# Attention, experts and a Strassen network on one core: conversions one operation at a time, four of them in the network, x split in halves

## The chip, the cores and the metric

The kernel runs on one core of a Trainium2 chip. The metric is the device time of one execution in microseconds (us). Five engines work side by side, each through its own instructions in the order in which they are recorded: TensorE (PE; its weight loads are PEld), VectorE (DVE), ScalarE (ACT), GpSimd (POOL) and SyncE (SP, which issues most DMAs). An instruction starts when its engine has finished the one before and when what it waits for is there.

## The reference, cut to what matters

```python
x = attention(q, k, v, tau)                 # 4 batches, 8 heads, 576 positions, width 64
x = x.reshape(2304, 512)
e = argmax(xn @ en.T / tau)                 # one of 8 experts for each token, gate g
y = relu(x @ w1[e]) @ w2[e]                 # w1: 512 x 1024, w2: 1024 x 512 for each expert
h = (g * y) @ w_in                          # 512 x 2048
out = (max(h, 0) + alpha * min(h, 0)) @ w_out   # 2048 x 512
```

The inputs are float64 in memory; w_in and w_out come to the core as pairs of 32-bit words, and have to be turned into a high and a low part.

## The kernel before, in words

The program has three stretches. **Attention** takes the first 345 us; the change does not touch it. **Experts** (function `experts`, to about 609 us) goes through 64 steps g, eight for each expert. In a step PE makes twelve products of the first layer (`l1`, L1225) and twelve of the second (`l2`, L1256 to L1258) for the step before. Each product is made of three matmuls (high by high, high by low, low by high), so every operand is split: ACT copies the high part, DVE or POOL subtracts the low one (`wsplit`, L1123/L1124 and L1137/L1138; `relu`, L1208 and L1209; `xprep`, L1175/L1176). `l2` waits for L1209, the low part of h.

Between them the same engines prepare the network. `conv` (L1620) turns a 128 x 512 block of w_in or w_out into 32-bit numbers: one ACT operation (L1605), five on DVE (L1606, L1607, L1609, L1613, L1614), and for w_in one POOL addition (L1646), for w_out an ACT copy (L1612) and two POOL operations (L1617, L1618). `CVG` lists the steps g at which one starts; it is a generator, and the loop decides how much of it is recorded at a time. There are 16 blocks of w_in and four of w_out. `early` is a list of due steps: sums and splits of w_in's blocks (`sums`, `factor`), the loads of x (`fetch`), its differences and splits (`diff`, `split`), on tiles of 128 x 768.

**The network** (function `near_network`, 609 to 1010 us) multiplies x by w_in in Strassen's way, with seven products (`PROD`) in place of eight. It makes six visits (`VISITS`): a visit takes one third q of the tokens and one half h of the 16 blocks f of the hidden width, in four pairs i. In a pair PE makes seven products of six matmuls (`prod`, L1869) into the banks ha and hb, and four groups of nine matmuls of the second layer (`f2mm`, L1985 to L1987). ACT copies ha away (`held`, L1878), DVE adds (L1891), `act` applies the leaky relu (ACT L1895/L1896 and DVE L1897, or in visits 3 to 5 DVE alone, L1900/L1902), ACT makes the high part gh (L1913) and POOL the low part gl (L1918). PE can go on with ha only when ACT has copied it.

Beside this stand chains of small steps: `tick` records after each PE group the next steps of each chain, as far as a budget for each engine allows (`room`); a step "N" does nothing and costs a place, and a change of engine within a chain costs one too. `finish` records what is left of a chain at once, where its result is needed. Chains are `wout` (a block of w_out, due in a certain pair), `factors` (the products' weights of one pair of w_in, with stores to DRAM, L2041, L2045, L2047), and at the end of visits 0, 1, 3 and 4, when x moves to another third, the differences and splits of the next x (`after`, `xsplit`). At the very end three blocks of the second layer's rows are stored by indirect DMAs that POOL issues (`put`, L1950).

Of the kernel before, what the change touches and what calls it, by code (L numbers as in the profile page):

```python
# [44 lines left out]
CVG = {False: [21 * i // 8 for i in range(KF2 + 4)], True: [4 * i for i in range(15)] + [59, 61]}  # L45
# [7 lines left out]
NV = 4  # L53
# [159 lines left out]
def attn_moe_ffn(ctx: ExitStack, tc, q, k, v, tau, emb, mtau, w1, w2, w_in, w_out, alpha, out):  # L213
# [843 lines left out]
    def experts(CAPS, general, y2):  # L1057
# [466 lines left out]
        for g in range(NE * KF + 1):  # L1524
# [3 lines left out]
            wsplit(1, g + LA1)  # L1528
            for x in todo:
                for _ in x:  # L1530
                    pass
            todo = []
# [25 lines left out]
    def shared(st, general):  # L1558
# [61 lines left out]
        def conv():  # L1620
# [12 lines left out]
            for group in ((0,), (1, 2, 3), (4,) if hl is not None else ()):  # L1633
                for x in group:
                    steps[x]()
                if group:
                    yield
            for x in steps[5 if hl is not None else 4:]:
# [83 lines left out]
        def diff(p, eng):  # L1722

            b11, b21, b12, b22 = raws()
            if p < 3:
                RAW["t", p] = t = cv_p.tile([128, KD // 2 * HB], F32, tag=f"t{p}", name=f"t{p}", bufs=1)
            if p == 1:
                eng.tensor_tensor(t, b12, b11, op=ALU.subtract)
            elif p == 2:
                eng.tensor_tensor(t, b22, RAW["t", 1], op=ALU.subtract)  # L1730
            elif p == 3:
                eng.tensor_tensor(b12, b22, b12, op=ALU.subtract)
            else:
                eng.tensor_tensor(RAW["t", 2], b21, RAW["t", 2], op=ALU.subtract)

        def split(p, eng):
            b11, b21, b12, b22 = raws()
            src = {1: b11, 2: b21, 6: RAW.get(("t", 2)), 7: b12, 5: RAW.get(("t", 1)), 3: b22, 4: RAW.get(("t", 2))}[p]
# [3 lines left out]
            yield  # L1742
            eng.tensor_tensor(t[:, 1], src, t[:, 0].bitcast(F32), op=ALU.subtract)
# [18 lines left out]
        for i in range(NQH):  # L1762
            g0 = 10.5 * i + 4.0
# [12 lines left out]
        for x, (kind, p, e) in enumerate((("s", 1, V), ("d", 1, G), ("s", 2, G), ("d", 3, V), ("d", 2, G), ("s", 7, V),  # L1776
                                          ("s", 6, V), ("s", 5, G), ("d", 4, G))):
            if kind == "d":
                at(g0 + 0.75 * x, lambda p=p, e=e: diff(p, e))
            else:  # L1780
                f = run(lambda p=p, e=e: split(p, e))
                at(g0 + 0.75 * x, f)
                at(g0 + 0.75 * x + 0.8, f)
# [534 lines left out]
```

## Time and profile before

| what | value |
| --- | --- |
| three timed runs | 1019.30, 1016.85 and 1019.21 us, median 1019.21 us |
| the profiled execution's own time | 1021.06 us |
| its span (first to last instruction) | 1019.2 us |
| mean granted TensorE clock | 0.981 |
| busy: PE, PEld, DVE, ACT, POOL | 961.3, 887.6, 797.7, 618.6, 684.9 us |

A row of the timeline reads: start and duration in us, engine, line, operation, what it writes and reads, how many; in brackets the engine's idle time before it and what ended that. A row of the waits reads: the waiting instruction, who it waited for, us in total, how many times, the longest. The rows that matter stand in the section below.

### The profile page before, as it was taken

How to read it: one execution, taken by the hardware profiler on the slowest of the kernel's cores; microseconds unless marked ns; L12 is line 12 of the kernel's file. 1: busy time of each engine (PE TensorE's matmuls, PEld its weight loads, DVE VectorE, ACT ScalarE, POOL GpSimd, SP SyncE). 2: the span in 40 equal slices, each digit the busy share in tenths (PEclk: the TensorE clock that was granted, in tenths of full speed). 3: DMA queues.
4: the chain of work that ended last, by engine and by line, in shares of the span. 5: the costliest groups of instructions: out<-in, count | busy, mean ns of one | idle time of the engine just before them, and what ended most of it. 6: DMA issues, size and time to landing. Idle time of an engine off the chain costs nothing. (4 is left out here: it accounts for less than half of the span.)

```text
span 1019.2 us, 18395 instructions
## 1 busy us (share of the span) xinstructions
PE 961.3 (94%) x6099; PEld 887.6 (87%) x6099; DVE 797.7 (78%) x1431; ACT 618.6 (61%) x1419; POOL 684.9 (67%) x654
## 2 busy tenths in 40 slices
PE   7999999899999599998998999999899999999995
PEld 6899999899999499998997998989788888798884
DVE  7999999999999688988999777874963567738633
ACT  6989999799998345655556456665565523324120
POOL 6988899899998433655889465747764647636523
PEclk7999999999999799999999999999999999999998
DMA  2333555534451477988989766557476655464641
GB/s 74 104 95 82 140 153 180 162 105 134 123 156 65 167 272 246 319 272 265 280 271 262 244 170 194 191 193 266 157 270 215 233 164 167 156 216 146 195 135 66
DMA packets 119160, 186.06 MB, mean 183 GB/s; under 512 B 24024, under 2 KB 50936, under 8 KB 119056
## 3 DMA queue, kind: packets, MB, share of 16 engines
q1 hardware_dynamic: 115184, 174.48, 55.1%
q0 software_dynamic: 3456, 9.59, 2.5%
q8 instruction: 51, 0.84, 0.3%
q10 hardware_dynamic: 416, 0.72, 0.2%
q14 instruction: 53, 0.43, 0.1%
HBM read 127.48 MB, written 48.41 MB: 173 GB/s over the span
## 5 line engine op out<-in xcount | busy, mean ns | idle before, releaser
L1918 POOL TENSOR_TENSOR gl<-c,gh 128x384 fp32r<-128x384 f32 x96 | 109.1, 1140 | 139.9 <-ACT gh L1913 122.1
L446 POOL TENSOR_TENSOR ptl<-x,pth 128x512 fp32r<-128x512 f32 x97 | 124.8, 1288 | 6.8
L1869 PE MATMUL ha<-x,wr 128*128 128x384 f32 x576 | 119.1, 342 | 5.9 <-ACT d L1878 3.9
L650 DVE SCALAR_TENSOR_TENSOR p<-s,mx,e 128x576 f32<-128x576 f32 x144 | 116.6, 812 | 7.2 <-ACT mx L638 3.2
L1987 PE MATMUL o<-wo,gl 128*128 128x512 f32 x288 | 115.2, 400 | 4.0 <-POOL gl L1918 4.0
L1869 PEld LDWEIGHTS ha<-x,wr 128*128 128x128 f32 x576 | 104.3, 190 | 16.6 <-ACT d L1878 5.5
L1225 PE MATMUL l<-x,w 128*128 128x256 f32 (+6 forms) x744 | 118.7, 308 | 0.0
L1986 PE MATMUL o<-wo,gh 128*128 128x512 f32 x288 | 114.7, 398 | 2.2 <-POOL wo L1618 2.2
L634 DVE TENSOR_REDUCE mx<-s 128x1 f32<-128x576 f32 x144 | 108.5, 754 | 8.3 <-PE s L627 5.2
L663 PE MATMUL t<-ident,p 128*128 128x128 f32 (+1 forms) x720 | 112.3, 277 | 2.2 <-ACT x L689 0.9
L1985 PE MATMUL o<-wo,gh 128*128 128x512 f32 x288 | 113.6, 394 | 0.0
L1225 PEld LDWEIGHTS l<-x,w 128*128 128x128 f32 x744 | 110.7, 188 | 0.6
L643 ACT ACTIVATE e<-s,mx 128x576 f32<-128x576 f32 x144 | 106.3, 739 | 7.1 <-DVE mx L634 6.0
L1869 PE MATMUL hb<-x,wr 128*128 128x384 f32 x432 | 87.8, 338 | 2.4 <-DVE c L1891 2.3
L1913 ACT CAST gh<-c 128x384 fp32r<-128x384 f32 x96 | 48.9, 514 | 66.5 <-DVE c L1902 47.0
L663 PEld LDWEIGHTS t<-ident,p 128*128 128x128 f32 (+1 forms) x720 | 81.1, 138 | 8.5 <-DVE p L650 2.4
L1257 PE MATMUL y<-h,w 128*128 128x256 f32 (+6 forms) x256 | 80.4, 314 | 6.9 <-DVE h L1209 6.7
L627 PE MATMUL s<-ks,qs 128*128 128x288 f32 x256 | 82.7, 338 | 2.4 <-ACT qs L534 1.4
L1208 ACT ACTIVATE h<-l 128x256 fp32r<-128x256 f32 (+6 forms) x64 | 28.3, 442 | 92.3 <-PE l L1225 90.7
L1256 PE MATMUL y<-h,w 128*128 128x256 f32 (+6 forms) x256 | 82.3, 321 | 2.0 <-ACT yT L1268 1.6
L1869 PEld LDWEIGHTS hb<-x,wr 128*128 128x128 f32 x432 | 76.9, 190 | 3.8 <-DVE c L1891 3.7
L1258 PE MATMUL y<-h,w 128*128 128x256 f32 (+6 forms) x256 | 79.1, 309 | 0.0
(274 smaller groups left out, 2649.1 us busy)
## 6 DMA issues: line engine op xcount, KB each, us to landing
wr<-ws SPq DMA_DIRECT2D x168, 256.0 KB
stg<-in_moe_w_dram SPq DMA_DIRECT2D x34, 512.0 KB
stg<-in_moe_w_dram SPq DMA_DIRECT2D x15, 1024.0 KB
kx<-ks SPq DMA_DIRECT2D x60, 144.0 KB
xd<-zt SPq DMA_DIRECT2D x33, 256.0 KB
raw<-yt_d SPq DMA_DIRECT2D x10, 768.0 KB
ws<-wr SPq DMA_DIRECT2D x28, 256.0 KB
ws<-wf SPq DMA_DIRECT2D x28, 256.0 KB
```

Source lines behind the costliest of these rows:

```text
L446: lambda: nc.gpsimd.tensor_tensor(lo, raw, hi.bitcast(F32), op=ALU.subtract))
L627: nc.tensor.matmul(s[:, hf, 0:288], lt, st[nm, a][:, hf * 288:(hf + 1) * 288], start=(j == 0 and x == 0), stop=(j == n - 1 and x == 1))
L634: nc.vector.tensor_reduce(out=mx[:, 0:1], in_=st["s", t][:, :, 0:288], op=ALU.min, axis=AX.XY)
L643: nc.scalar.activation(e, st["s", t][:, :, 0:288], AF.Exp, bias=st["mx", t][:, 0:1], scale=-1.0)
L650: nc.vector.scalar_tensor_tensor(out=p.rearrange("q (a b) -> q a b", a=2), in0=st["s", t][:, :, 0:288], scalar=st["mx", t][:, 2:3], in1=st ...
L663: nc.tensor.transpose(m[0:w, j * n + i * 128:j * n + (i + 1) * 128], st["p", t][:, c * 128:c * 128 + w], ident)
L1225: nc.tensor.matmul(m[:, 0:n], w[:, a, c], st["x"][:, b, c, 0:n], start=(i == 0), stop=(i + 1 == len(terms)))
L1869: nc.tensor.matmul(m, w[:, a, k], x[:, b, k], start=start and n == 0, stop=n + 1 == len(terms), skip_group_check=not start)
L1918: P.tensor_tensor(gl, c, gh.bitcast(F32), op=ALU.subtract)
L1985: nc.tensor.matmul(m, gh[:, ts], WO[f][:, 0, :], start=first and x == 0, stop=False)
L1986: nc.tensor.matmul(m, gh[:, ts], WO[f][:, 1, :], start=False, stop=False)
L1987: nc.tensor.matmul(m, gl[:, ts], WO[f][:, 0, :], start=False, stop=n[0] == full and x + 1 == len(gs))
```

## The change

In the experts a conversion is recorded one operation at a time, two places in a step g, instead of in runs of three and two or more; 16 start there instead of 20, every 3.33 steps instead of every 2.63. Four blocks of w_in (c = 12 to 15) are converted in the network instead, by a new chain `win` in visits 1 and 2. The sums and splits of w_in's blocks come at other steps. In the network, differences and splits of x are made in halves; differences 1 to 3 for the next x move to DVE and start a pair earlier, and difference 4 goes into another tile. The chain behind `act` gets one more empty step before the high part. In the last two pairs of visits 3 and 4 `act` uses the form with two ACT operations. Blocks of w_out start at other pairs. At the end the last three high and low parts are recorded before the groups that lead to the stores.

```diff
-CVG = {False: [21 * i // 8 for i in range(KF2 + 4)], True: ...}
+CVG = {False: [10 * i // 3 for i in range(16)], True: ...}
...
             for x in todo:
-                for _ in x:
-                    pass
-            todo = []
+                next(x, None)
...
             if g in CVG[general]:
                 todo.append(conv())
-                next(todo[-1])
-                next(todo[-1])
...
+            if not general:
+                for x in todo:
+                    next(x, None)
...
-            cvq = [(1, 2 * i + x) for h in range(NQH) for i in (h, NQH + h) for x in range(2)] + [(2, c) for c in range(NV)]
+            cvq = [(1, 2 * i + x) for i in (0, NQH, 1, NQH + 1, 2, 3) for x in range(2)] + [(2, c) for c in range(NV)]
...
+            for n, x in enumerate(steps):
                 x()
-            cvload()
+                if n == (5 if hl is None else 6):
+                    cvload()
+                yield
...
-        def diff(p, eng):
+        def diff(p, eng, half):
...
+            o, x, y = {1: (t1, b12, b11), 2: (t2, b22, t1), 3: (b12, b22, b12), 4: (b11, b21, t2)}[p]
+            n = slice(half * HB, (half + 1) * HB)
+            eng.tensor_tensor(o[:, n], x[:, n], y[:, n], op=ALU.subtract)
...
             nc.scalar.copy(t[:, 0], src)
-            yield
-            eng.tensor_tensor(t[:, 1], src, t[:, 0].bitcast(F32), op=ALU.subtract)
+            for half in range(2):
+                yield
+                n = slice(half * HB // 2, (half + 1) * HB // 2)
+                eng.tensor_tensor(t[:, 1, :, n], src[:, :, n], t[:, 0, :, n].bitcast(F32), op=ALU.subtract)
...
-            g0 = 10.5 * i + 4.0
+            g0 = (8.0, 21.0, 34.5, 45.0)[i]
...
-            if v < 3:
+            if v < 3 or busy:
...
-            chain(0, first + join + [("A", 0.52, halves), ("P", 1.12, low)], ("g", v, f, hf), 1)
+            chain(0, first + join + [("N", 0, nothing), ("A", 0.52, halves), ("P", 1.12, low)], ("g", v, f, hf), 1)
...
+        def win(c):
...
+            chain(3, [("W", 0, lambda: len(open_) < 2), ("S", 0, load)] + [("N", 0, nothing)] * 3 + [("A", 0.67, begin)]
+                  + [("V", t, lambda k=k: x["steps"][k + 1]()) for k, t in enumerate((0.75, 0.75, 1.2, 0.5, 0.75))]
+                  + [("P", 1.4, add), ("N", 0, nothing), ("S", 0, store)], ("c", c))
...
-                if i == NQH - 2 and p == 1:
+                if i == 1 and p == 1:
...
-                          + [("N", 0, nothing)] * 5 + [("P", 2.15, lambda: diff(1, P)), ("V", 1.0, lambda: diff(3, V)),
-                                                       ("P", 2.15, lambda: diff(2, P))], "fetch")
+                          + [("N", 0, nothing)] * 5 + [x for d in (1, 3, 2) for half in range(2) for x in (
+                              ("V", 0.6, lambda d=d, half=half: diff(d, V, half)), ("N", 0, nothing))], "fetch")
...
-        work = {0: [("o", NV + x, 0) for x in range(NQH)], 1: [("f", NQH, 0), ("f", NQH + 1, 2)] + [("o", 8 + x, x) for x in range(3)],
-                2: [("f", NQH + 2, 0), ("f", NQH + 3, 2), ("o", 11, 0), ("o", 12, 3)], 3: [("o", 13, 0), ("o", 14, 1), ("o", 15, 2)]}
+        work = {0: [("o", NV, 0), ("o", NV + 1, 0), ("o", NV + 2, 1), ("o", NV + 3, 2)],
+                1: [("f", NQH, 0), ("c", 2 * NQH + 4, 0), ("f", NQH + 1, 1), ("c", 2 * NQH + 5, 1), ("o", 8, 2)],
+                2: [("f", NQH + 2, 0), ("c", 2 * NQH + 6, 0), ("c", 2 * NQH + 7, 0), ("o", 9, 1), ("o", 10, 1), ("f", NQH + 3, 2),
+                    ("o", 11, 2), ("o", 12, 3)],
+                3: [("o", 13, 0), ("o", 14, 1), ("o", 15, 2)]}
...
+                busy = moving(v) and i >= 2
...
+        for f, hf in ((f1, 1), (f0, 1), (f1, 0)):
+            finish(("g", v, f, hf))
         f2mm(v, (f1,), 1)
         f2mm(v, (f0,), 1)
```

The first place is DVE in the experts, expert 5 (272 tokens), around one conversion of w_out; x7s is the conversion's tile, h the low part that PE waits for. Before:

```order
L1138 TENSOR_TENSOR w2_8273<-stg2_8111,w2_8273 128x512
L1606 TENSOR_SCALAR x7s_8294<-x7s_8294 128x512
L1607 TENSOR_SCALAR x7s_8294<-x7s_8294 128x512
L1609 SCALAR_TENSOR_TENSOR x7s_8294<-x2s_8058,x7s_8294 128x512
L1209 SCALAR_TENSOR_TENSOR h_8312<-l1_8299,h_8312 128x272
L1124 TENSOR_TENSOR w1_8315<-stg1_8054,w1_8315 128x512
L1613 TENSOR_SCALAR x7s_8294<-x7s_8294 128x512
L1614 SCALAR_TENSOR_TENSOR x7s_8294<-x2s_8058,x7s_8294 128x512
L1176 TENSOR_TENSOR x0_8216<-x_8325,x0_8216 128x320
L1209 SCALAR_TENSOR_TENSOR h_8368<-l1_8355,h_8368 128x272
```

And now:

```order
L1616 TENSOR_SCALAR x7s_8170<-x7s_8170 128x512
L1176 TENSOR_TENSOR x0_8137<-x_8195,x0_8137 128x320
L1138 TENSOR_TENSOR w2_8201<-stg2_8041,w2_8201 128x512
L1617 TENSOR_SCALAR x7s_8170<-x7s_8170 128x512
L1209 SCALAR_TENSOR_TENSOR h_8238<-l1_8225,h_8238 128x272
L1124 TENSOR_TENSOR w1_8241<-stg1_7987,w1_8241 128x512
L1619 SCALAR_TENSOR_TENSOR x7s_8170<-x2s_7941,x7s_8170 128x512
L1176 TENSOR_TENSOR x0_8137<-x_8245,x0_8137 128x320
L1209 SCALAR_TENSOR_TENSOR h_8289<-l1_8276,h_8289 128x272
L1124 TENSOR_TENSOR w1_8292<-stg1_7987,w1_8292 128x512
L1623 TENSOR_SCALAR x7s_8170<-x7s_8170 128x512
```

Three operations of the conversion stood together ahead of one h; now one or two stand between one h and the next.

The second place is POOL in the last pair of visit 0. wo7 is the block of w_out that PE needs first in the next visit, x2 and x5 are splits, t2 and raw the targets of difference 4. Before:

```order
L1743 TENSOR_TENSOR x2_9690<-raw_9495,x2_9690 128x768
L1918 TENSOR_TENSOR gl_9714<-c_9670,gh_9713 128x384
L1617 TENSOR_TENSOR f_9540<-f_9540,wo7_9542 128x512
L1734 TENSOR_TENSOR t2_9642<-raw_9495,t2_9642 128x768
L1743 TENSOR_TENSOR x5_9746<-t1_9596,x5_9746 128x768
L1918 TENSOR_TENSOR gl_9788<-c_9742,gh_9787 128x384
L1918 TENSOR_TENSOR gl_9802<-c_9768,gh_9801 128x384
L1618 TENSOR_TENSOR wo7_9542<-f_9540,r_9541 128x512
L1918 TENSOR_TENSOR gl_9839<-c_9784,gh_9838 128x384
```

And now:

```order
L1627 TENSOR_TENSOR f_9523<-f_9523,wo7_9525 128x512
L1932 TENSOR_TENSOR gl_9641<-c_9579,gh_9640 128x384
L1745 TENSOR_TENSOR raw_9291<-raw_9291,t2_9520 128x384
L1932 TENSOR_TENSOR gl_9655<-c_9593,gh_9654 128x384
L1756 TENSOR_TENSOR x2_9674<-raw_9291,x2_9674 128x2x192 x2
L1932 TENSOR_TENSOR gl_9697<-c_9637,gh_9696 128x384
L1745 TENSOR_TENSOR raw_9291<-raw_9291,t2_9520 128x384
L1756 TENSOR_TENSOR x5_9720<-t1_9386,x5_9720 128x2x192 x2
L1628 TENSOR_TENSOR wo7_9525<-f_9523,r_9524 128x512
L1932 TENSOR_TENSOR gl_9776<-c_9715,gh_9775 128x384
L1932 TENSOR_TENSOR gl_9796<-c_9743,gh_9795 128x384
```

The last operation on wo7 (L1618, now L1628) stands ahead of the two gl that it stood behind. Differences 1 and 2, which POOL made shortly before (L1728, L1730), are gone from its order.

The third place is ACT at the start of visit 0, from the copy of ha that follows the fifth product. Before:

```order
L1878 COPY d_9248<-ha_9185 128x384
L1913 CAST gh_9253<-c_9211 128x384
L1605 ACTIVATE f_9256<-cr_9198 128x512
L1895 ACTIVATE u_9269<-ha_9185 128x384
L1896 ACTIVATE c_9268<-ha_9185 128x384
L1895 ACTIVATE u_9251<-c_9250 128x384
```

And now:

```order
L1892 COPY d_9215<-ha_9150 128x384
L1615 ACTIVATE f_9220<-cr_9163 128x512
L1615 ACTIVATE f_9224<-cr_9165 128x512
L1909 ACTIVATE u_9237<-ha_9150 128x384
L1910 ACTIVATE c_9236<-ha_9150 128x384
L1927 CAST gh_9250<-c_9176 128x384
```

The first gh stood directly behind the copy; now four operations come first, two of which wait for PE's sixth product.

## Rows read from the trace of the kernel before

**Rows 1.** The page, busy time of PE: us, share of the span, instructions.
```profile
PE 961.3 (94%) x6099; PEld 887.6 (87%) x6099; DVE 797.7 (78%) x1431; ACT 618.6 (61%) x1419; POOL 684.9 (67%) x654
```
**Rows 2.** Waits of PE in the network, 600 us to the end.
```profile
PE o L1987 <- POOL gl L1918: 4.0, 3, 3.1
PE ha L1869 <- ACT d L1878: 3.9, 3, 1.8
PE hb L1869 <- DVE c L1891: 2.3, 3, 1.1
PE o L1986 <- POOL wo L1618: 2.2, 1, 2.2
PE ha L1869 <- DVE c L1902: 2.0, 2, 1.3
```
**Rows 3.** Waits of PE in the experts, 400 to 600 us.
```profile
PE y L1257 <- DVE h L1209: 6.5, 7, 1.5
PE y L1256 <- ACT yT L1268: 1.6, 1, 1.6
PE y L1256 <- ACT w L1137: 0.4, 1, 0.4
```
**Rows 4.** Windows: stretch, length, busy PE, PEld, DVE, ACT, POOL, clock, DMA, GB/s.
```profile
470.00:490.00 20.00, 16.39 (x125) 15.60 (x124) 19.66 (x35) 10.11 (x23) 10.71 (x10) 1.00 0.80 252
...
670.00:680.00 10.00, 7.78 (x31) 6.53 (x30) 5.69 (x7) 5.05 (x10) 5.54 (x4) 0.83 0.36 138
...
750.00:760.00 10.00, 8.23 (x35) 7.39 (x34) 5.75 (x9) 8.25 (x18) 4.55 (x5) 0.83 0.85 293
...
750.00:800.00 50.00, 48.23 (x233) 43.12 (x232) 22.11 (x36) 28.91 (x65) 23.93 (x26) 0.97 0.72 239
```
**Rows 5.** Timeline of the experts, around two of PE's waits for h.
```profile
474.73 1.20 DVE L1295 TENSOR_TENSOR be<-be,sm 128x64 f32<-128x64 f32 x1
...
476.57 0.38 PE L1257 MATMUL y<-h,w 128*128 128x256 f32 x1 [1.51 <-DVE h L1209]
...
542.90 1.70 DVE L1609 SCALAR_TENSOR_TENSOR x7s<-x2s,x7s 128x512 uint32<-128x512 uint32 x1
...
545.00 0.39 PE L1257 MATMUL y<-h,w 128*128 128x272 f32 x1 [1.51 <-DVE h L1209]
```
**Rows 6.** Timeline of visits 0 to 2, the steps that hold PE up.
```profile
646.14 2.29 POOL L1728 TENSOR_TENSOR t<-raw 128x768 f32<-128x768 f32 x1
...
671.25 1.58 POOL L1618 TENSOR_TENSOR wo<-f,r 128x512 fp32r<-128x512 f32 x1
...
716.90 2.60 DVE L1732 TENSOR_TENSOR raw<-raw 128x768 f32<-128x768 f32 x1
...
750.21 0.40 ACT L2041 CAST wf<-sum 128x256 fp32r<-128x256 f32 x1 [2.23 <-DMA ws<-wf]
```
**Rows 7.** Timeline of the end.
```profile
999.53 0.51 ACT L1913 CAST gh<-c 128x384 fp32r<-128x384 f32 x1 [1.75 <-DVE c L1902]
...
1002.12 0.98 POOL L1950 DMA_INDIRECT out_dram<-os,gs  x1 [0.30 <-DVE os L1931]
...
1004.38 1.02 POOL L1918 TENSOR_TENSOR gl<-c,gh 128x384 fp32r<-128x384 f32 x1
1005.46 0.79 PE L1987 MATMUL o<-wo,gl 128*128 128x512 f32 x1 [3.14 <-POOL gl L1918]
...
1011.12 0.97 POOL L1950 DMA_INDIRECT out_dram<-os,gs  x1 [0.41 <-POOLq L2281]
```
**Rows 8.** Groups of equal instructions in the network: us busy, mean ns of one.
```profile
L1918 POOL TENSOR_TENSOR gl<-c,gh 128x384 fp32r<-128x384 f32 x96 | 109.1, 1140 | 139.9 <-ACT gh L1913 122.1 <-PE hb L1869 14.0 <-PE ha L1869 2.0
```
**Rows 9.** Timeline of visit 0's start.
```profile
612.25 0.56 DVE L1891 TENSOR_TENSOR c<-hb,v 128x384 f32<-128x384 f32 x1 [1.71 <-PE hb L1869]
...
612.75 0.96 DVE L1743 TENSOR_TENSOR x<-raw,x 128x768 fp32r<-128x768 f32 x1
...
617.33 0.49 ACT L1895 ACTIVATE u<-ha 128x384 f32<-128x384 f32 x1 [0.42 <-PE ha L1869]
```
**Rows 10.** Timeline of the end, POOL's low part and PE's use of it.
```profile
995.74 1.01 POOL L1918 TENSOR_TENSOR gl<-c,gh 128x384 fp32r<-128x384 f32 x1 [5.06 <-ACT gh L1913]
...
997.26 0.39 PE L1987 MATMUL o<-wo,gl 128*128 128x512 f32 x1
```

More of the change, by code (lines that the diff above doesn't have):

```diff
@@ L43 @@
 WARM2 = 18
-CVG = {False: [21 * i // 8 for i in range(KF2 + 4)], True: [4 * i for i in range(15)] + [59, 61]}
+CVG = {False: [10 * i // 3 for i in range(16)], True: [4 * i for i in range(15)] + [59, 61]}
 CV2 = (8, 14, 20)
@@ L1551, in experts @@
                 todo.append(conv())
-                next(todo[-1])
-                next(todo[-1])
+                if general:
+                    next(todo[-1])
+                    next(todo[-1])
+            if not general:
+                for x in todo:
+                    next(x, None)
+        for x in todo:
+            for _ in x:
+                pass
         for i in range(len(ntile(NE - 1))):
@@ L1882, in near_network, with act @@
         acts = []
-        def act(v, f, hf, m, w=None):
+        def act(v, f, hf, m, w=None, busy=False):
             if len(acts) > 2:
@@ L2021, in wout, with load, begin, add @@
                   + [(e, t, lambda k=k: nth(k + 1)) for k, (e, t) in enumerate(kinds)], ("wo", c))
+        def win(c):
+            x = {}
+            def load():
+                open_.append(("c", c))
+                x["raw"] = raw = cw_p.tile([128, 1024], U32, tag="cr", name="cr", bufs=2)
+                nc.sync.dma_start(raw.rearrange("p (k f) -> p k f", k=2), y2["cvsource"](1, c))
+            def begin():
+                f, r = x["fr"] = [cw_p.tile([128, 512], U32, tag=nm, name=nm, bufs=2) for nm in ("f", "r")]
+                x["steps"] = [y[2] for y in y2["cvsteps"](x["raw"], f, r, None)]
+                x["steps"][0]()
+            def add():
+                f, r = (t.bitcast(F32) for t in x["fr"])
+                P.tensor_tensor(f, f, r, op=ALU.add)
+            def store():
+                i, half = divmod(c, 2)
+                nc.sync.dma_start(wa_d[i - NQH][:, half * DM:(half + 1) * DM], x["fr"][0].bitcast(F32))
+                open_.remove(("c", c))
+            chain(3, [("W", 0, lambda: len(open_) < 2), ("S", 0, load)] + [("N", 0, nothing)] * 3 + [("A", 0.67, begin)]
+                  + [("V", t, lambda k=k: x["steps"][k + 1]()) for k, t in enumerate((0.75, 0.75, 1.2, 0.5, 0.75))]
+                  + [("P", 1.4, add), ("N", 0, nothing), ("S", 0, store)], ("c", c))
         def factors(i):
@@ L2049, in next_ @@
                     made.remove(i)
-            steps = [("W", 0, lambda: not made), ("S", 0, load)] + [("N", 0, nothing)] * 3
+            steps = [("W", 0, lambda: not made and not any(x["name"] in (("c", 2 * i), ("c", 2 * i + 1)) for x in chains)),
+                     ("S", 0, load)] + [("N", 0, nothing)] * 3
             steps += [("V", 0.8, lambda k=k: nth(k)) for k in range(4)] + [("N", 0, nothing)]
@@ L2062, in hi @@
                 next(x["g"])
-            chain(2, [("A", 0.85, hi), (e, 1.05 if e == "V" else 2.15, lambda: next(x["g"], None))], ("x", p))
+            chain(2, [("A", 0.85, hi)] + [(e, 0.6 if e == "V" else 1.1, lambda: next(x["g"], None))] * 2, ("x", p))
         def moving(v):
@@ L2112, in near_network @@
                     if when == i:
-                        (wout if kind == "o" else factors)(x)
+                        {"o": wout, "f": factors, "c": win}[kind](x)
                 if h and q != VISITS[2][0] and i == NQH - 2:
@@ L2128, in near_network @@
                 prod(v, i, 2, b, True)
-                act(v, f0, 0, b, d1)
+                act(v, f0, 0, b, d1, busy)
                 step(2)
@@ L2140, in near_network @@
                 d3 = held("d", a)
-                act(v, f1, 1, b, d3)
+                act(v, f1, 1, b, d3, busy)
                 step(5)
```

55 lines of the change are left out of this document (29 added, 26 removed).

## The prediction

> **What bounds the kernel now.** I read the page's busy times first: PE is busy for 961.3 of 1019.2 us [rows 1]. No engine can shorten that work here, since the change removes no matmul; what can go is time in which PE waits, and time in which its clock is down. So I read next who ends PE's waits. In the network they sum to 4.0 + 3.9 + 2.3 + 2.2 + 2.0 = 14.4 us, in five groups of two or three waits each [rows 2]: a low part gl from POOL, a copy of ha from ACT, an addition on DVE, a block of w_out from POOL, and DVE's half of the activation. In the experts they are 8.5 us, 6.5 of them in seven waits for DVE's low part of h [rows 3]. Third, the windows: between 470 and 490 us DVE is busy 19.66 of 20 us, so there it is itself the bound; and two stretches of 10 us in the network have a granted clock of 0.83 [rows 4]. Those two hold the waits of 2.2 for w_out and of 1.8 for ACT's copy, and PE ran at the lower of its two levels for a while after each. A loss of 17% of 10 us is 1.7 us each, so 3.4 us more hang on these two waits. Together 14.4 + 8.5 + 3.4 = 26.3 us could go at most from these places, all but the stores behind PE's last work, which I take apart. Then I read single steps, to see what stands in front of each wait.
>
> **Experts.** Two waits of 1.51 us are the longest [rows 5]. At 545.00 the cause is a conversion's operation of 1.70 us right before the low part of h; it was one of three recorded together. The change leaves one or two between one h and the next, so this kind goes. At 476.57 it is `be`, a step of the mixing weights of 1.20 us, and its neighbours; these don't move, and while DVE is at 19.66 of 20 us a shorter run only hands the lateness on. I take the seven waits for h and the one for yT (ACT, whose w_out copy stood between DVE's operations), 8.1 us, and let 4.7 go: somewhat over half. The ends: nothing gained, if DVE is full throughout, and 7 us, if all but the wait on `be` (and the small one for w) goes. Four conversions fewer take work off DVE there; that is worth nothing by itself where PE isn't waiting, and its help is in the 4.7. **Gain 4.7 (0 to 7).**
>
> **The block of w_out (wo7).** PE waited 2.2 us for L1618 of 1.58 us at 671.25 [rows 6], with 1.7 us of clock behind it. In the new order this operation stands ahead of two gl that it stood behind, and differences 1 and 2, of which the row at 646.14 shows one with 2.29 us on POOL, are gone from that queue. The differences alone are up to 4.6 us, the wait was 2.2, so it goes whole. What is late next: the two gl behind it; PE has other groups to do before it needs them. **Gain 3.9 (0 to 3.9).**
>
> **ACT's copies of ha.** Three waits, 3.9 us, and 1.7 of clock behind the longest. That one comes from the factors: a copy into wf waited 2.23 us for a transfer, the store of the previous wf, and the copy of ha stood behind it on ACT [rows 6]. The change does not take the store away. It moves the chain's place, and adds traffic to visits 1 and 2: four loads of raw words and four stores, where the DMA engines already show 0.72 over 750 to 800 and 0.85 between 750 and 760 [rows 4]. Of 5.6 us I let 3.0 stand, half of the two shorter waits (2.1) and 2.0 of the longest with its clock: **gain 2.6 (-1.5 to 5)**, the lower end being one more such wait on a store with nothing else saved.
>
> **DVE's additions and activations at the ends of moving visits.** Five waits, 4.3 us. The row at 716.90 shows why: a difference of 128 x 768 took 2.60 us on DVE, and what PE needed stood behind it [rows 6]. Halves put at most half of this ahead of it, and in the last two pairs of visits 3 and 4 ACT takes two operations of the activation over from DVE. Against it stands that differences 1 and 2 now are DVE's. They start a pair earlier, where DVE has room (22.11 busy of 50 us between 750 and 800, a stretch without a moving x [rows 4]). **Gain 3.2 (0 to 4.3)**; the loss is a rival below.
>
> **The end.** Six stores are issued by POOL, and they set the last instruction: the first at 1002.12 took 0.98, the last begins at 1011.12. Between them POOL makes the gl for which PE waited 3.14 us, at 1004.38, 1.02 long, though its gh had begun at 999.53 and taken 0.51 [rows 7]. POOL's order put stores ahead of gl. The change records gl first: then it ends near 1001.1, and six stores follow, at steps of about 1.3 (0.98 and what lies between: an estimate, from 0.98 plus the 0.30 and 0.41 of idle time that these rows show). The last begins at 1001.1 + 5 x 1.3 = 1007.6 in place of 1011.12. PE's last groups would begin some 4 us earlier, so they don't take its place as the bound. **Gain 3.5 (2.5 to 4.7)**, the upper end if the stores are no longer held by anything but their issue.
>
> **What it costs.** First, the empty step behind `act` delays each of the 96 groups of gh and gl by a place. POOL's gl lasts 1.14 us on average and its queue mostly waits for gh (139.9 us of idle time) [rows 8], so POOL is not late by itself; the delay falls on the margin between gl and its use. At the start of visit 0 this margin is smallest: gh used to stand right behind a copy, and now four ACT operations come first, two of them, the casts of conversions, beside u and c, which wait for PE's next product (617.33 shows such a wait, 0.42 [rows 9]). I take 2.2 us there (0 to 4, the top being two waits of about 2: four operations of the 0.49 of that row). Second, elsewhere: at the end a gl was finished at 995.74 + 1.01 = 996.75 and used at 997.26, a margin of 0.5, with no first product between [rows 10]; in the steady pairs two products stand between, so most stay hidden. There I count with the four conversions that now lie in visits 1 and 2 (DVE five operations each, ACT and POOL one each, hidden in a DVE that is busy 44% of the time there) and with blocks of w_out that start later. I take 2.0 us for all of it (0 to 6; the top is one wait of 0.5 in each of about 12 pairs). Third, the halves: on DVE, 128 x 384 took 0.56 us and 128 x 768 took 0.96 [rows 9], so two halves cost 0.16 more; a visit's end has eight halved operations on DVE, and four ends make 32 x 0.16 = 5.1 us. I count it at nothing, hidden beside PE. If the cover is gone, it is paid. **Cost 4.2 (0 to 10).**
>
> The Trainium skill speaks against the halves: its page "Perfetto Trace Analysis", section "Optimizing Scalar/DVE Operations", says that grouping into larger operations improves throughput if the engine is saturated, and only where it is not, but causes bubbles elsewhere, does breaking instructions up help. The rows at 0.56 and 0.96 agree that a half costs more than half. By that rule, with DVE full at the visit ends, the sum would be 5.1 us higher; that case is in the second rival.
>
> **The sum.** 4.7 + 3.9 + 2.6 + 3.2 + 3.5 = 17.9, less 4.2, is 13.7 us. The profiled execution took 1021.06 us, so the changed kernel would take 1007.4 beside it; that execution lies 1.85 above the median of the three runs shown, 1019.21, and I forecast the median: **1005.5 us**.
>
> **Rivals.** *Nearly all waits go.* If the moved work lands in idle stretches everywhere, the gains come near their upper ends (7 + 3.9 + 5 + 4.3 + 3.5 = 23.7) with some 3 of cost: 20.7 less, 998.5. For it speaks that POOL and ACT are far from full; against it the wait on `be` and the one on the store, which stay. Chance 0.11.
>
> *The engines are full where it matters.* DVE at 19.66 of 20 us for a stretch of the experts, and again at visit ends, only shifts the lateness, and the 5.1 us of halves are paid. Then the experts give 1.5, wo7 3.9, ACT 1.5, DVE 3.2, the end 3.5: 13.6, less 4.2 and 5.1: 4.3; without the halves 9.4. Between these: 7 less, 1012.2. Chance 0.24.
>
> *DVE becomes the bound at the ends of visits 0, 1, 3 and 4: slower.* Differences 1 and 2 bring DVE 2 x 0.96 and the halves 1.3 us at each, 3.2 in all, and since DVE also stretched to 2.60 for one difference, they may cost more. If PE waits for all of it, and its clock falls each time as it did for 1.7 us, an end costs 3.2 + 1.7 = 4.9, four cost 19.6. The other terms leave 13.7 - 3.2 = 10.5, so the median comes to 1028.3. It decides from 10.5 / 4 = 2.6 us an end on. Without the clock, 12.8 against 10.5, it is 1021.5, within 0.3% of now. Against it: the differences start a pair earlier, and DVE is busy 78% on the whole [rows 1]. Chance 0.07 for slower, 0.08 for about no change (with the case that the new starts of gl eat up what the experts give).
>
> **How the numbers follow.** The forecast has 0.50, nearly all waits 0.11, full engines 0.24. About 0.3%, 3 us, is what a measurement of this kernel can tell from no change; all three cases are faster by more: 0.85, no change 0.08, slower 0.07. The range of 8 in 10 runs from 998 (the first rival) to 1015 (the second without most of its gain); what lies above is no change and slower.
>
> **What would show it.** Right: no wait over 1 us for h but at the mixing weights; no wait for w_out behind visit 0 and a clock near 1 there; the last store beginning within 6.5 us after its gl; PE busy as before, 961 us, so that the time won is idle time lost. Wrong: waits for gl in the first pair of visit 0 above 4 us, or scattered over all pairs; waits for DVE at the ends of visits 0, 1, 3 and 4 above 2.6 us each; DVE still at 98% around 470 to 490 with the same waits for h. If the last store still begins 9 us behind the first, the order at the end was not the reason.

## The result and the profile after

| | median | range | against before |
| --- | --- | --- | --- |
| before | 1019.25 us | 1016.85 to 1020.41 | |
| changed | 1008.54 us | 1006.63 to 1009.50 | 0.9897, interval 0.9880 to 0.9914 |

The change gains 10.7 us; 13.7 were forecast (a median of 1005.5), and 1008.54 lies in the range. The profiled execution took 1008.70 us (span 1006.9), against 1021.06 (1019.2) before: 12.3 us of span. PE's busy time on the page of the changed kernel is 1.1 us less than before [rows 1], so 11.2 of the 12.3 us were idle time of PE:

```profile
PE 960.2 (95%) x6099; PEld 889.6 (88%) x6099; DVE 811.4 (81%) x1461; ACT 633.0 (63%) x1451; POOL 673.3 (67%) x663
```

PE's waits in the experts of the changed kernel, 400 to 600 us (who waits for whom, us in total, times, longest), to set beside [rows 3]; and under the line of dots those from 600 us to the end, beside [rows 2]:

```profile
PE y L1257 <- DVE h L1209: 5.2, 4, 3.0
PE y L1256 <- ACT h L1208: 0.6, 1, 0.6
...
PE o L1999 <- ACT gh L1927: 2.4, 3, 1.3
PE ha L1883 <- ACT c L1910: 2.2, 1, 2.2
PE o L2001 <- POOL gl L1932: 1.1, 3, 0.4
PE ha L1883 <- ACT d L1892: 0.6, 1, 0.6
PE hb L1883 <- DVE c L1905: 0.5, 1, 0.5
```

The wait for w_out is gone, the one of 3.1 us for the last gl is gone, DVE's c went from 4.3 us to 0.5. New are a wait of 3.0 for h, waits for gh, and one of 2.2 for ACT's c.

PE executes the same 6099 matmuls in the same order in both kernels. So the n-th of one trace can be set against the n-th of the other, and the difference of their starts, followed along the program, is a ledger of where time went (negative: the changed kernel is ahead):

| stretch (time before) | gained or lost there | stands at the end |
| --- | --- | --- |
| experts to 556 us | -6.2 | -6.2 |
| 556 to 579, a wait of 3.04 for h and a slow clock behind it | +5.0 | -1.2 |
| start of visit 0 (614 to 623), five waits for d, gh and gl | +2.1 | +0.9 |
| wo7, end of visit 0 (673 to 677) | -4.0 | -3.1 |
| start of visit 1 (706), a wait for gh | +2.2 | -0.9 |
| visit 1 (720 to 756), waits for c and d that went | -6.3 | -7.2 |
| visit 2 (758), a wait of 2.2 for ACT's c, and the clock | +4.2 | -3.0 |
| visit 2, a wait for gl | -0.7 | -3.7 |
| ends of visits 3 and 4 | -4.4 | -8.1 |
| the end (from 1005) | -4.2 | -12.3 |

The windows of the changed kernel (columns as in [rows 4]) show the two slow stretches, 0.66 in the experts and 0.83 in visit 2, and that the stretch of wo7, 670 to 680, now runs at 1.00. In 470 to 490 DVE is as full as before, but PE is busy 18.35 in place of 16.39. The two rows under the dots are the ends of visits 0 and 1, of which more below:

```profile
470.00:490.00 20.00, 18.35 (x136) 17.75 (x135) 19.82 (x37) 11.87 (x27) 11.54 (x11) 1.00 1.03 325
550.00:560.00 10.00, 6.96 (x29) 6.71 (x28) 8.94 (x11) 2.29 (x5) 5.82 (x6) 0.66 0.54 173
670.00:680.00 10.00, 10.00 (x51) 8.95 (x50) 8.23 (x13) 6.24 (x12) 3.52 (x4) 1.00 0.72 265
750.00:760.00 10.00, 7.78 (x31) 6.28 (x30) 5.53 (x9) 6.05 (x14) 5.74 (x6) 0.83 0.93 322
...
655.00:676.00 21.00, 21.00 (x106) 18.95 (x105) 19.11 (x22) 15.42 (x29) 16.56 (x14) 1.00 0.55 167
720.00:742.00 22.00, 21.50 (x106) 18.80 (x105) 21.01 (x24) 15.15 (x30) 16.25 (x14) 1.00 0.51 161
```

The new wait in the experts, on PE's timeline of the changed kernel and, under the dots, on DVE's:

```profile
553.50 0.63 PE L1257 MATMUL y<-h,w 128*128 128x320 f32 x1 [3.04 <-DVE h L1209]
...
546.78 3.82 DVE L1124 TENSOR_TENSOR w<-stg,w 128x512 fp32r<-128x512 f32 x1
...
550.97 2.08 DVE L1617 TENSOR_SCALAR x6s<-x6s 128x512 uint32<-128x512 uint32 x1
552.97 0.48 DVE L1209 SCALAR_TENSOR_TENSOR h<-l,h 128x320 fp32r<-128x320 f32 x1
553.37 0.68 DVE L1124 TENSOR_TENSOR w<-stg,w 128x512 fp32r<-128x512 f32 x1
```

and on POOL's:

```profile
546.79 1.31 POOL L1627 TENSOR_TENSOR x7s<-x7s,wo 128x512 f32<-128x512 f32 x1
548.03 1.31 POOL L1138 TENSOR_TENSOR w<-stg,w 128x512 fp32r<-128x512 f32 x1
549.29 0.74 POOL L1698 TENSOR_TENSOR sum<-wa,sum 128x256 f32<-128x256 f32 x1
550.20 1.26 POOL L1386 DMA_INDIRECT pd<-sm,ysl_i  x1 [0.16 <-issue]
551.48 1.27 POOL L1628 TENSOR_TENSOR wo<-x7s 128x512 fp32r<-128x512 f32 x1
```

The same split takes 0.68 us at 553.37, where POOL does nothing, and 3.82 at 546.78, beside three POOL operations that follow each other without a gap. The Trainium skill, "SBUF — State Buffer", section "Who interferes with whom", says that a DVE instruction with two inputs from SBUF contends with a GpSimd instruction that reads SBUF; the rows agree. A second operation ahead of the same h was slow too: the TENSOR_SCALAR at 550.97, of one input, took 2.08 us beside POOL's indirect DMA and L1628, where the same one took 0.43 in the run with later sums below (551.24).

In the network the new waits begin on ACT. Five rows of its timeline:

```profile
703.19 0.40 ACT L2084 CAST wf<-sum 128x256 fp32r<-128x256 f32 x1 [2.72 <-DMA ws<-wf]
703.50 0.51 ACT L1927 CAST gh<-c 128x384 fp32r<-128x384 f32 x1
...
752.02 0.40 ACT L2084 CAST wf<-sum 128x256 fp32r<-128x256 f32 x1 [3.61 <-DMA ws<-wf]
752.33 0.48 ACT L1909 ACTIVATE u<-ha 128x384 f32<-128x384 f32 x1
752.71 0.48 ACT L1910 ACTIVATE c<-ha 128x384 f32<-128x384 f32 x1
```

A copy into wf waits for the store of the tile's old contents, and gh (703.50) or the reading of ha (752.33, 752.71) stands behind it. The end, on POOL's timeline, beside [rows 7]:

```profile
991.97 1.02 POOL L1932 TENSOR_TENSOR gl<-c,gh 128x384 fp32r<-128x384 f32 x1 [1.09 <-ACT gh L1927]
993.14 1.00 POOL L1964 DMA_INDIRECT out_dram<-os,gs  x1 [0.15 <-DVE os L1945]
...
999.57 0.98 POOL L1964 DMA_INDIRECT out_dram<-os,gs  x1 [0.30 <-issue]
```

### The profile page after: what moved, and what is told of

Same layout as the page of the kernel before. It is cut to its first block, busy times and chain, and to the rows that moved or that the text cites. A ratio compares the mean times of both kernels' runs of the same rounds, so it can differ in the third digit from the quotient of the medians.

```text
span 1006.9 us, 18456 instructions
## 1 busy us (share of the span) xinstructions
PE 960.2 (95%) x6099; PEld 889.6 (88%) x6099; DVE 811.4 (81%) x1461; ACT 633.0 (63%) x1451; POOL 673.3 (67%) x663
## 5 line engine op out<-in xcount | busy, mean ns | idle before, releaser
L1138 POOL TENSOR_TENSOR w<-stg,w 128x512 fp32r<-128x512 f32 x28 | 38.4, 1371 | 65.6 <-ACT w L1137 62.3
```

## The experiments

Each is timed against the kernel before on its own chip. For comparison, the changed kernel has the ratio 0.9897; differences from it are worked out as (ratio / 0.9897 - 1) x 1008.5 us. Offsets "in the trace" are those of the ledger, here against the changed kernel. The intervals of three experiments (the order at the end, all 20 conversions, the fourth pair's sums) overlap the changed kernel's, and that of the differences on POOL touches it; for those the timing alone would hardly show a difference. A single trace has a spread of its own: four of the kernels below (the first, second and fourth, and four buffers alone) execute the same instructions as the changed kernel in the experts, and there their traces come out 1.3, 2.8, 4.6 and 1.7 us ahead of it. In the fourth the wait at 553 us is missing, and one of 1.64 stands at 540.

### The order at the end undone

```diff
-        for f, hf in ((f1, 1), (f0, 1), (f1, 0)):
-            finish(("g", v, f, hf))
```

> Undoes one part of the change: the last three gl are again recorded where the groups need them, behind stores in POOL's order. Theory (the order of gl and stores sets the end): all before 990 us as in the changed kernel, PE waits about 3 us for the last gl again, the last store begins some 9 us behind the first; 4 us slower, about 1012.5 us. Rival (the stores run at the pace of PE's last groups, whatever stands between them): within 1 us of the changed kernel, 1007.5 to 1009.5.

Measured: 1011.15 us, ratio 0.9924 (0.9904 to 0.9944), 2.8 us slower than the changed kernel. In the trace nothing differs by over 2.2 us before the end, and there PE waits 3.1 us for gl again and falls 4.9 us behind (its profiled execution, 1013.58, was the slowest of six). POOL's timeline of this kernel:

```profile
995.38 0.97 POOL L1964 DMA_INDIRECT out_dram<-os,gs  x1 [0.30 <-issue]
996.37 1.01 POOL L1932 TENSOR_TENSOR gl<-c,gh 128x384 fp32r<-128x384 f32 x1
999.08 0.99 POOL L1964 DMA_INDIRECT out_dram<-os,gs  x1 [1.70 <-DVE os L1945]
...
1003.35 0.97 POOL L1964 DMA_INDIRECT out_dram<-os,gs  x1 [0.74 <-POOLq L2331]
```

The theory holds: gl behind a store, PE behind gl, the next store (999.08) behind PE's result. The first store lies at 992.81, the last 10.5 us behind it; in the changed kernel it is 6.4 (993.14 to 999.57).

### No empty step ahead of gh

```diff
-first + join + [("N", 0, nothing), ("A", 0.52, halves), ...
+first + join + [("A", 0.52, halves), ...
```

> Undoes one part: the empty step ahead of each high part gh is gone. Theory (it only delays gh, and is paid at the start of visit 0): the five waits at 614 to 625 us (2.5 us) shrink to the two of the kernel before (0.9), nothing else changes; 1.5 to 2 us faster, about 1006.7. Rival (the empty step is what lets ACT copy ha ahead of gh in the steady pairs, so that the waits for ACT's copy went through it): PE's waits for ACT's copies come back, 2 us or more in sum beside the gain at the start; 1008.5 to 1011.

Measured: 1001.50 us, ratio 0.9840 (0.9817 to 0.9862), 5.8 us faster than the changed kernel: more than either side expected. In the trace the start of visit 0 gives 2.1 us, as the theory had it, but the place at 704 gives 2.2 more and the one at 753 another 1.2. The waits from 600 us on:

```profile
PE o L2001 <- POOL gl L1932: 1.1, 2, 0.8
PE ha L1883 <- ACT c L1910: 0.9, 1, 0.9
PE ha L1883 <- ACT d L1892: 0.6, 1, 0.6
PE hb L1883 <- DVE c L1905: 0.5, 1, 0.5
```

All waits for gh are gone, and no wait for ACT's copies came back, so the rival falls. (Another 2.8 us of the trace's difference lie in the experts, which this edit does not touch; more on them at the end.)

### Conversions in runs again

```diff
-                next(x, None)
+                for _ in x:
+                    pass
+            todo = []
...
-                if general:
+                for _ in range(2 if general else 4):
                     next(todo[-1])
...
-            if not general:
-                for x in todo:
-                    next(x, None)
```

> Undoes one part: in the experts a conversion is again recorded in runs (four operations, then the rest a step later), at the 16 places of the changed kernel. Theory (runs on DVE were not the main cause; what holds DVE's low part of h up is POOL's work beside it, as at 546.78 us, where a split of 0.68 us took 3.82): the waits for h in the experts stay within 2 us of the changed kernel's 5.2 in sum; median within 2 us, 1007 to 1010.5. Rival (runs were the cause): six or more waits for h, 9 us or more in sum in the experts; 4 to 6 us slower, 1012.5 to 1014.5.

Measured: 1001.53 us, ratio 0.9844 (0.9823 to 0.9865), 5.4 us faster. It undoes what I had put down for a gain, and neither side expected it to be faster by that much. One row of its waits in the experts:

```profile
PE y L1257 <- DVE h L1209: 3.0, 3, 1.7
```

The waits for h are 3.0 us against 5.2, none is over 1.7, and the clock does not fall; in the trace the experts gain 6.4 us. So runs on DVE were not the cause. The windows from 380 to 600 us of the changed kernel and of this one show what the spreading did:

```profile
380.00:600.00 220.00, 214.10 (x1444) 208.68 (x1443) 183.47 (x267) 122.76 (x277) 133.96 (x117) 0.98 0.78 251
...
380.00:600.00 220.00, 216.83 (x1492) 212.06 (x1491) 175.90 (x270) 125.67 (x281) 140.62 (x121) 1.00 0.77 252
```

DVE does three operations more in this run and is busy 7.6 us less: single operations were stretched more often. That POOL's work does the stretching is tested further below. The edit also moves operations to other places, which by the last experiment is worth some us by itself.

### Differences 1 and 2 on POOL again

```diff
-                              ("V", 0.6, lambda d=d, half=half: diff(d, V, half)), ("N", 0, nothing))], "fetch")
+                              ("V" if d == 3 else "P", 0.6 if d == 3 else 1.1,
+                               lambda d=d, half=half: diff(d, V if d == 3 else P, half)), ("N", 0, nothing))], "fetch")
```

> Undoes one part: differences 1 and 2 of the next x are POOL's again at the moving visits, in halves and at the new places. Theory (wo7 came early mostly because these two left POOL's queue): PE waits 1.5 to 2.5 us for wo7's last step at the start of visit 1 again, with a clock that falls behind it; 2 to 5 us slower, 1010.5 to 1013.5. Rival (the new places, a pair earlier, are enough, and wo7 goes by its place ahead of two gl): no wait for w_out; DVE has 2 x 2 x 0.56 us less at each end; within 1 us or up to 2 us faster, 1006.5 to 1009.5.

Measured: 1010.51 us, ratio 0.9935 (0.9914 to 0.9956), 3.9 us slower. The time is what the theory said, the place is not. In the trace it falls 5.4 us behind in the network, while the experts, which are the same, were 4.6 faster in this one execution. Its waits from 600 us on begin with

```profile
PE o L1999 <- ACT gh L1927: 5.3, 2, 4.4
PE o L2001 <- POOL gl L1932: 3.4, 4, 2.4
```

and there is none for w_out: wo7 is early by the new places alone, its own ahead of two gl and the differences' a pair earlier, which are not told apart here. (Difference 3 was DVE's before the change too.) The loss has two places. About 2 us of it lie at 704: POOL's two differences delay gl, as this stretch of its timeline shows, with a wait of PE of 2.4 us that ends with the row at 699.41:

```profile
695.55 1.33 POOL L1745 TENSOR_TENSOR t<-raw 128x384 f32<-128x384 f32 x1
696.85 1.61 POOL L2053 TENSOR_TENSOR f<-f,r 128x512 f32<-128x512 f32 x1
...
699.41 1.31 POOL L1932 TENSOR_TENSOR gl<-c,gh 128x384 fp32r<-128x384 f32 x1
```

The other 3.6 lie between 750 and 765, at the wait of 4.4 us for gh. There ACT stood 4.32 and 3.65 us on the store of an old wf (3.61 in the changed kernel), as for the second of them these rows show:

```profile
752.91 0.41 ACT L2084 CAST wf<-sum 128x256 fp32r<-128x256 f32 x1 [3.65 <-DMA ws<-wf]
...
755.28 0.93 ACT L1927 CAST gh<-c 128x384 fp32r<-128x384 f32 x2
```

Why these stores are later here is not shown. At the ends of visits 3 and 4 this edit changes nothing (under 0.3 us from 840 us on), so what was won there does not hang on the differences' engine.

### Differences and low parts whole again

```diff
-            for half in range(2):
-                yield
-                n = slice(half * HB // 2, (half + 1) * HB // 2)
-                eng.tensor_tensor(t[:, 1, :, n], src[:, :, n], t[:, 0, :, n]..., op=ALU.subtract)
+            yield
+            eng.tensor_tensor(t[:, 1], src, t[:, 0]..., op=ALU.subtract)
```

(and `diff` likewise, whole in its first half).

> Undoes one part: differences and low parts of x are whole again (128 x 768), at the same engines and, within a place or two, the same places. Theory (DVE has room at the ends of visits; halves cost it 5.1 us that nobody waits for, and shorten what stands ahead of PE's additions): without them one or two waits for DVE's c of 0.4 to 1 us come back; 0 to 3 us slower. Rival (more instructions cost time on full engines): 2 to 5 us faster.

Measured: 1009.73 us, ratio 0.9906 (0.9887 to 0.9925): 0.9 slower, not distinguishable from the changed kernel by the timing. In the trace it falls 1.5 us behind. All of that arises at 706, where the granted clock is 0.79 from 704 to 712 us (1.00 in the changed kernel); the trace of the first experiment, whose edit is elsewhere, loses as much there at the same clock. There are two waits for DVE's c (0.7 us) in place of one (0.5). So what the halves bring is too small to show. They cost DVE 8.8 us of busy time (811.4 against 802.6 on the pages), which cost nothing that shows either.

### All 20 conversions in the experts again

```diff
-CVG = {False: [10 * i // 3 for i in range(16)], ...
+CVG = {False: [21 * i // 8 for i in range(20)], ...
...
-            g0 = (8.0, 21.0, 34.5, 45.0)[i]
+            g0 = 10.5 * i + 6.0
...
-                1: [("f", NQH, 0), ("c", 2 * NQH + 4, 0), ("f", NQH + 1, 1), ("c", 2 * NQH + 5, 1), ("o", 8, 2)],
-                2: [("f", NQH + 2, 0), ("c", 2 * NQH + 6, 0), ("c", 2 * NQH + 7, 0), ("o", 9, 1), ("o", 10, 1), ("f", NQH + 3, 2),
+                1: [("f", NQH, 0), ("f", NQH + 1, 1), ("o", 8, 2)],
+                2: [("f", NQH + 2, 0), ("o", 9, 1), ("o", 10, 1), ("f", NQH + 3, 2),
```

(and the old order of the list `cvq`).

> Undoes one part: all 20 conversions in the experts again (at the steps of the kernel before, one operation at a time, sums at the old distance), none of w_in in the network. Theory (the experts' waits come from DVE and POOL lying over each other, and four conversions more there make more of it): 2 to 6 us slower in the experts; in the network 1 to 4 us faster, since the four conversions' loads and stores no longer delay the store of wf; 1006 to 1013 us. Rival (moving them out was the change's gain): 8 us or more slower in the experts, nothing back in the network.

Measured: 1012.07 us, ratio 0.9921 (0.9904 to 0.9938), 2.4 us slower; 5.1 in the trace, of which 1.3 lie before 386 us, ahead of the conversions, and 3.7 in the experts, where nine waits for h sum to

```profile
PE y L1257 <- DVE h L1209: 8.2, 9, 1.7
```

The experts' half of the theory came out in size. But the edit also moves every conversion and the sums to other steps, and a shift of one step alone is worth some 2.5 us (last experiment), so the four conversions more and the other places are not told apart. The network gave nothing back (waits at 693, 702 and 777 us took the place of those at 704 and 753): ACT's longest wait for a store of wf is even 4.9 us, so it is not the four conversions' traffic that makes these stores late.

### Two parts undone together, and more buffers for wf

> Two parts undone together, each of which alone was 5 to 6 us faster than the changed kernel: runs in the experts and no empty step ahead of gh. Theory (they are paid at different places, the experts at 553 us and the network's first pairs and 704 us): the gains add up, of 7 us in the experts and 5 in the network; 995 to 998 us, ratio to before about 0.979. Rival (in both runs it was the same thing, a clock that happened not to fall in the experts): no more than 1001 us, ratio 0.984, like each alone.

Measured: 997.96 us, ratio 0.9808 (0.9783 to 0.9833). It is the edits of the second and the third experiment. The gains add up: in the trace 6.4 us in the experts and 5.5 in the network (1.1 is lost before 386 us, where nothing was changed). With the buffers as well:

```diff
-        y2["wf"] = npool("wf", bufs=3)
+        y2["wf"] = npool("wf", bufs=4)
-        g_p = npool("g", bufs=6)
+        g_p = npool("g", bufs=5)
```

> The run before it with four buffers for the factors' tiles wf in place of three (and five in place of six for gh and gl, to make room). Theory (ACT stands 2 to 3.6 us on the store of an old wf, and with it gh, c and the copies of ha that PE needs): ACT's waits on that store fall below 1 us, PE's waits between 690 and 760 us (0.9 + 0.8 without the empty step) go; 1 to 3 us faster than the run before it. Rival (the transfers are late by the load on the DMA engines, and one more buffer only moves the wait on): ACT's waits stay, within 1 us.

Measured: 996.24 us, ratio 0.9774 (0.9758 to 0.9790). No wait of ACT on that store is left, and the two waits of PE at 743 and 747 us (1.5 us) shrink to one of 0.4; 1.5 us in the trace, as the theory said. The intervals overlap a little, so the timing alone would not show it.

### Four buffers for wf alone

> The changed kernel, empty step and single operations kept, with four buffers for wf in place of three (five in place of six for gh and gl). Theory (what PE loses at 704 and 753 us, 2.2 and some 4 us with the clock, starts at ACT's waits of 2.7 and 3.6 us for the store of an old wf): both waits and what PE loses behind them go, the start of visit 0 keeps its 2.5 us; 4 to 6 us faster than the changed kernel, about 1003. Rival (the empty step alone makes gh late there, as the gain without it at 704 and 745 us suggests): PE still waits at 704 for gh; within 2 us.

The edit is that of the buffers above, on the changed kernel. Measured: 1001.20 us, ratio 0.9848 (0.9825 to 0.9872), 5.0 us faster. ACT's waits for the store in the changed kernel,

```profile
ACT wf L2084 <- DMA ws<-wf: 10.9, 6, 3.6
```

and with four buffers, with what PE still waits for gh:

```profile
PE o L1999 <- ACT gh L1927: 1.5, 3, 0.9
...
ACT wf L2084 <- DMA ws<-wf: 1.5, 2, 0.8
```

In the trace the places at 704 and 753 give 5.2 us; the five waits at the start of visit 0 stay at 2.5. So the losses at 704 and 753 need two things at once: a gh or a reading of ha that stands behind a copy into wf, most often because of the empty step, and a store that is late. The buffers alone take away all 5.2 us; taking out the empty step takes 3.4, and the buffers then add 1.5. What makes the stores late stays open.

### The fourth pair's sums three steps later

```diff
-            g0 = (8.0, 21.0, 34.5, 45.0)[i]
+            g0 = (8.0, 21.0, 34.5, 48.0)[i]
```

> The changed kernel with the sums and splits of w_in's fourth pair three steps later, so that three of POOL's additions no longer lie beside the DVE split at 546.78 us, which took 3.82 us in place of 0.68. Theory (a DVE operation with two inputs from SBUF does not go on while POOL works back to back, and this made PE's wait of 3.04 us and the half clock behind it): that split takes 2.7 us or less, the wait at 553 falls below 2 us and the clock stays up; 4 to 6 us faster, about 1003.5. Rival (DVE is simply full there, 10 us of work in a step of 6): the wait stays within 0.5 us, or comes back in full a step later; within 2 us.

Measured: 1003.94 us, ratio 0.9870 (0.9853 to 0.9888), 2.8 us faster; 4.0 in the trace from the experts. Of these the run without the empty step gained 2.8 there without any edit, its clock having held, so some 1.2 are left for the edit itself. The split and the waits:

```profile
547.84 2.49 DVE L1124 TENSOR_TENSOR w<-stg,w 128x512 fp32r<-128x512 f32 x1
```

```profile
PE y L1257 <- DVE h L1209: 3.7, 3, 1.6
```

DVE has the same operations in the same order. Only POOL's work, and ACT's copies that belong to it, lie elsewhere; the split takes 2.49 in place of 3.82, PE's wait behind it 0.6 in place of 3.04 (one of 0.38 ahead of it grew to 1.57), and the clock holds. A DVE that is "simply full" would not have moved: the two waits are 2.2 us in place of 3.4. That the clock held need not be the edit's doing.

### The fastest version, twice varied

First with the sums of the experiment before it; then, without them, with every conversion a step later (`10 * i // 3 + 1` in `CVG`).

> The fastest version so far (runs in the experts, no empty step, four buffers for wf) with the later sums as well. Theory: its wait of 1.72 us at 547 us lies beside POOL's additions too and goes or halves; 0 to 2 us faster than 996.2. Rival: the sums meet the next conversions and make a new wait there; 0 to 2 us slower.

Measured: 993.06 us, ratio 0.9766 (0.9751 to 0.9782), the best of the study: 24 us less than before on its chip, and by the ratios 13 less than the changed kernel. Its waits of PE in the experts:

```profile
PE y L1257 <- DVE h L1209: 2.5, 3, 1.3
```

Against the version without the later sums its span is 3.2 us less, but 2.2 of that lie before 420 us, where the edit moves nothing; the wait of 1.72 us went to 1.30, and some 1 us is the edit's. The two intervals overlap.

> The fastest version so far with every conversion of the experts one step later, nothing else changed. Theory (what is left there, 0.94 us at 474 and 1.72 at 547, is a run of three that meets the mixing weights or POOL's additions, by coincidence of places): the two waits change by over 0.5 us each, in either direction, the sum of waits for h lies anywhere from 0.5 to 6 us. Rival (the waits come from the amount of work): the sum stays at 3.0 within 0.7.

Measured: 996.83 us, ratio 0.9799 (0.9785 to 0.9814), about 2.5 us slower than unshifted. The wait of 0.94 us became 1.85, that of 1.72 went, others of 1.63 and 0.74 came: 4.6 us for h in sum (3.0 before the shift) and 0.8 for yT. The same work, one step later, makes other waits: places decide at this size. The amount of work was not varied here.

## Why the prediction was right, and where not

The direction, the range and the nature of the gain (idle time, PE's work the same) were right. That the sum came near is in part luck, since terms up to 4 us off in both directions cancelled. Of the gains only the order at the end was undone by itself and came back at its place; the others are read from the ledger and the waits that went. Of the signs set out ahead, no wait for w_out and a clock of 1.00 behind visit 0 came true. The wait of 3.04 us for h, away from the mixing weights, is one that should not have been there; and the last store begins 6.6 us after the last gl ends (992.99 to 999.57), where 6.5 was the limit. By the steps:

- **The block of w_out: 3.9 forecast, 4.0 in the ledger.** The size was right and half of the reason was not: without the differences' leaving POOL (the fourth experiment) there is no wait for wo7 either. The new places were enough.
- **The end: 3.5 forecast, 4.2 in the ledger; 2.8 by the timed reversal.** Order of gl and stores, as put; the stores follow each other at 1.28 us, where 1.3 was estimated.
- **The start of visit 0: -2.2 forecast, -2.1.** Right in place and cause. For the empty step elsewhere I put down late gl (2.0 with all else that was new). What it cost elsewhere was 3.4 us at 704 and 753, by another path: it put gh and the readings of ha behind the copies into wf, which I had on the list of the ACT waits without joining the two. Those 3.4 are part of the losses of the next step.
- **ACT's copies: 2.6 forecast, about -1.4** (the two waits of 1.54 and 1.76 with their clock went, some 5 us; the losses at 704 and 753 came, 6.4). This is one failed step: I took the wait on a store as one that persists at 2 us, and the range's lower end (-1.5) for "one more such wait". There were two, of 2.72 and 3.61.
- **Experts: 4.7 forecast, 1.2.** The other failed step. By 556 us 6.2 us were won, near the upper end of 7; then 5 were lost in one place. "One or two between one h and the next, so this kind goes" took the length of the run on DVE for the cause. The durations in [rows 5] (1.70 for an operation that takes 0.68 at 553.97 us in the changed kernel's timeline) showed already that it was stretched, and in that trace POOL worked beside it, from 542.28 to 544.04. Spreading the operations shortened the runs and stretched the operations; undone, the kernel is 5.4 us faster. With runs, 16 conversions and the sums at their new steps the experts gain 7.6 us on the kernel before, so what the change won there came from the fewer conversions and the new places, which no run tells apart. The 5.0 lost at one place are those of one execution; the same instructions lost 2.8 less in the second experiment's trace, where the clock held, and 4.6 less in the fourth's, where the wait itself is missing.
- **DVE at the visits' ends: 3.2 forecast, some 5.5.** The ends of visits 3 and 4 alone gave 4.4; why more than the waits for c of [rows 2] stays open. The halves (fifth experiment) and the differences' engine (fourth) make nothing of it that shows; the earlier start and the two ACT operations of the activation were not tested by themselves. The rival in which DVE becomes the bound there did not come about: one wait of 0.5 is left. The Trainium skill, "Perfetto Trace Analysis", section "Optimizing Scalar/DVE Operations", says that larger operations "can improve throughput if the engine is saturated"; weighed ahead, that would have cost 5.1 us. At the ends of visits 0 and 1 DVE is busy 19.11 of 21 and 21.01 of 22 us, close to full, and whole operations were no faster all the same, as PE waits there only 0.5 us in all. (The 0.56 us of [rows 9] is an addition that reads hb, not a half.)
- **Four conversions moved: their cost in the network counted as hidden, their help as part of the experts' 4.7.** Undone together with the places, 2.4 us by the timing, 3.7 in the experts of the trace; in the network nothing came back, so the cost there was hidden as far as the trace shows.

So the forecast sum of 13.7 (12.3 in the profiled executions, 10.7 by the medians) has two terms too high by 3.5 and 4; those on DVE and the end were too low by 2.3 and 0.7, and of the 2.0 put down for gl being late in the other pairs nothing showed outside the places named.

## What to carry to other kernels

A wait behind an operation that takes several times its usual duration was here a matter of what another engine did at that moment, not of how many operations stood in the row: compare the duration with the same operation's elsewhere before moving anything. A step that is delayed "by a place" is cheap or dear by what it then stands behind on its engine: look for instructions there that wait for a transfer. And when a change is made of many parts, undo them one at a time: two of these cost over 5 us each and hid behind the gains of the rest.

## What was not expected of the hardware

PE's clock does not fall after every wait of the same length at the same place. In the changed kernel the wait of 3.04 us at 553.50 is followed by a granted clock of 0.72 from 552 to 564 us:

```profile
552.00:564.00 12.00, 10.50 (x52) 10.28 (x53) 10.09 (x13) 5.19 (x12) 7.00 (x6) 0.72 0.59 221
```

Without the empty step, whose experts are the same, a wait of 3.05 us at 553.82 is followed by 1.00:

```profile
552.00:564.00 12.00, 10.18 (x68) 9.96 (x69) 11.53 (x14) 6.72 (x15) 8.01 (x7) 1.00 0.67 231
```

What decides it stays open; such a place makes a trace differ by some 2 to 3 us without any edit, so the ledger was read place by place. And a DVE operation on 128 x 512 took 3.1 us more than its 0.68 beside three POOL operations in a row.
